# Two chunks of 256 tokens beside the first MLP become one of 512 with its output in two passes

## The chip, the cores and the metric

The kernel runs on one core of a Trainium2 chip. The metric is the device time of one execution in microseconds; each version is run several times and the median is given.

## The reference, cut to what matters

```python
def _attn_ref(q, k, v, omega):             # q, k, v: (4, 8, 576, 64), omega: (128, 64)
    ...
    q_p, k_p = (phi(q_s), phi(k_s))        # random features with exp
    kv = np.einsum('bhsm,bhsd->bhmd', k_p, v)
    z = np.sum(k_p, axis=2)
    num = np.einsum('bhsm,bhmd->bhsd', q_p, kv)
    den = np.einsum('bhsm,bhm->bhs', q_p, z)[..., None] + 1e-06
    return (num / den).astype(np.float32)

def _moe_ref(x, w_in, w_out, alpha):       # x: (2304, 512), d_ff 2048
    h = x @ w_in
    g = np.maximum(h, 0.0) + alpha * np.minimum(h, 0.0)
    return (g @ w_out).astype(np.float32)

def _moe2_ref(x, w_a, w_b, w_out):         # d_ff 1536
    ...
    return (a * b @ w_out).astype(np.float32)
```

The result is attention, then the first MLP, then the second, for 2304 tokens of 512 features, all in float32. The change lies in the first MLP alone.

## The kernel before, in words

Every float32 matrix product is made of three products of high and low halves: a value's high half is its float32r rounding, made on ScalarE (`xh`, `gh`, the high half of a weight), its low half is the value less that, made on VectorE or POOL (`xl`, `gl`). TensorE sums high x high, high x low and low x high.

The first MLP has 16 tiles of 128 hidden features, numbered f, in two phases of 8. Phase 0 takes f 0 to 7 for all tokens and writes partial sums to the memory tile `ypart`; phase 1 takes f 8 to 15, reads `ypart` (`load_y`, line 652), adds and writes it back. For one chunk of tokens and one f, `h` is 12 matmuls (4 tiles of input features, 3 products each); ScalarE takes `u` from it, VectorE multiplies and adds (`u<-u,bend,h`), ScalarE makes `gh`, VectorE `gl`; `y` is another 12 matmuls into four output tiles, which stand in PSUM until the last f.

In phase 0 the first 1280 tokens are five chunks of 256 (`CI`, `NCI`), worked on while attention still runs; `work0` (lines 1107 and 1108) lists them. Chunks 0 and 1 are done by `A.run`. From there `group` (line 1048) sets the order of work, written out by hand: a group is two steps of attention (projections `pp`, `kv`, `nd` for numerator and denominator, transposes `tp` and `xp`, with their copies) and up to two items of the list `line`: the `y` of the pair before, put between the transposes, then two `h` (`Mlp.whole`, line 576). `whole` leaves the making of `gh` and `gl` to a list `after` that the next group flushes in its middle. When attention has no steps left, `h` and `y` alternate without it. The last y of a chunk leaves PSUM through a tile `yo` of the pool `io`, which has one buffer (line 499), and a store on SP's queue (lines 638 to 644).

After the last chunk `over()` (line 1100) closes attention's pools, opens the pools of the 512-token stage and issues its first two splits, `xh_1280_0`, `xl_1280_0`, `xh_1280_1`, `xl_1280_1`; only then is the last `y` of the chunk at token 1024 popped from the queue (lines 1171 and 1172). The stage for tokens 1280 to 2303 and phase 1 follow, then the second MLP.

The weights come as float32 bits in DRAM and are decoded into halves by `Decoder`. During the chunks of 256 there are 17 free slots for decoded weights (`NS1`); further ones open with the 512-token stage.

Of the kernel before, what the change touches and what calls it, by code (L numbers as in the profile page):

```python
# [9 lines left out]
F32 = mybir.dt.float32  # L10
F32R = mybir.dt.float32r
# [7 lines left out]
P = 128  # L19
# [39 lines left out]
PACE3 = 1  # L59
FIRST = 32  # L60
ALONE = 4
LAND = 5.0
SIDE = 0

# [2 lines left out]
def tile_kernel(ctx: ExitStack, tc: tile.TileContext, qT, kT, v1, omT, wbits, alpha, out):  # L67
# [145 lines left out]
    class Decoder:  # L213
# [255 lines left out]
    def hilo(q):  # L469
        D_.upto(q)  # L470
        return slots[place(q)][:2]
# [5 lines left out]
    class Mlp:  # L477
# [98 lines left out]
        def whole(self, ph, o, n, f, last):  # L576
# [18 lines left out]
            self.after.append(rest)  # L595
            self.q.append((self.a_back, ph, o, n, f, last))

        def a_back(self, ph, o, n, f, last_chunk):
# [12 lines left out]
            gh, gl = self.gs.pop((ph, o, f))  # L611
            for e in range(KT):
                es = slice(e * P, (e + 1) * P)
                head = not self.pair or e % 2 == 0
                tail = not self.pair or e % 2 == 1
                for i, (w_, r_) in enumerate(((wh, gh), (wh, gl), (wl, gh))):
                    tensor.matmul(ys[e], lhsT=w_[:, es], rhs=r_,
                                     start=(first and i == 0 and head), stop=(last and i == 2 and tail))
                if not self.pair and e < 3 and not last:
                    D_.fill()  # L620
            D_.free[2 * f + 1] = last_chunk
            if last:
# [386 lines left out]
    with st_m:  # L1009
# [35 lines left out]

        wait = {}

        def group(fronts, at):

            s = nxt_s[0]  # L1050
            nxt_s[0] += 2
            D_.step(2 * DEC1)
# [12 lines left out]
            if kv:  # L1065
                a_kv(*kv.pop(0))
            spread(fronts, KT)
# [10 lines left out]
            spread(line[at:at + 5], 2)  # L1078
            D_.go(5)
            for i in range(2):  # L1080
                if i < len(t):
                    a_t(*t[i])
                    wait["num"].append(t[i])
                if full:
                    A.back_one(fronts, 2 - i)
            for w in fronts:
                A.whole(*w)
                if not full:
                    A.back_one(fronts)
            D_.go(3)  # L1090

        def more():
            return nxt_s[0] < last_q or any(wait.values())
# [11 lines left out]


        work0 = [(0, CI * i, CI, fs, False) for fs in (range(NFH), range(NFH, NF0)) for i in range(2)]
        work0 += [(0, CI * i, CI, range(NF0), False) for i in range(2, NCI)]

        def ready(end, k):  # L1110
            b, t = divmod(end - 1, S)
# [32 lines left out]
                        most -= 1  # L1144

        i = sum(len(w[3]) for w in work0[:ALONE])
        while i < len(line):
            if not more():
                spread(line[i:i + 5], 2)
            pair = []  # L1150
            early = 1 if more() else 0
            for w in line[i:i + 2]:
                ph, o, n, f, _ = w
                if all((ph, o, k) in A.xs or x_there(o + n, k, True) for k in range(KT)) and D_.ready >= 2 * f + 2 - early:
                    pair.append(w)
            if len(pair) < 2 and more():
                pair = []
            if more():
                group(pair, i)
            else:  # L1160
                for w in pair:
                    A.flush()
                    A.whole(*w)
                    A.back_one(pair, 3)
                    D_.fill()
# [345 lines left out]
```

## Time and profile before

| | |
|---|---|
| median of 3 runs | 946.66 us (946.53 to 946.99) |
| the profiled execution | 947.25 us, span 945.5 us |
| mean granted clock of TensorE | 0.998 of full speed |
| busy share of the span | TensorE 98%, VectorE 65%, ScalarE 54%, POOL 13% |
| the chain that ended last | TensorE 93%, ScalarE 3%, VectorE 2% |

The span goes from the first to the last instruction of the profiled execution; its own time is 1.75 us longer. Busy shares are means over stages with different limits, so what a change in one stage is worth is read from that stage's waits. In the rows, PE is TensorE, DVE VectorE, ACT ScalarE, SPq the queue of SyncE; `L189` is a helper that records every matmul and most VectorE instructions, so groups are told apart by tile names.

### The profile page before, as it was taken

Reading aid. Unit: us, or ns where it says so; the run is one execution under the profiler, and the core shown is the slowest. Engines: PE = TensorE matmul, PEld = TensorE weight load, DVE = VectorE, ACT = ScalarE, POOL = GpSimd, SP = SyncE. Lnnn points to the kernel's source line nnn. Section 1 sums busy time; section 2 is a strip of 40 time slices with the busy share of each in tenths; the row PEclk is TensorE's granted clock in tenths of the full one; section 3 lists DMA queues with packets and bytes.
Section 4 is the critical chain, followed back from the end, with each engine's and each line's share of the span. In section 5 each row is a group of like instructions: output and inputs, shape, how many; then the busy total and the mean of one; then the engine's idle time right before and its main releaser. Section 6 shows DMA issues by size and latency. Waiting matters only on the chain.

```text
span 945.5 us, 16672 instructions
## 1 busy us (share of the span) xinstructions
PE 930.3 (98%) x6483; PEld 842.1 (89%) x6483; DVE 610.0 (65%) x1248; ACT 508.5 (54%) x1195; POOL 125.5 (13%) x107
## 2 busy tenths in 40 slices
PE   7989999999999999999999999999999999999998
PEld 6779999989888888889888999999999998989896
DVE  4987875653567677678776786866486833373633
ACT  5977766543455555445444556555465542444541
POOL 2786700000001202000000000000011111110201
PEclk9999999999999999999999999999999999999999
DMA  8444322000233352356546856159828368323323
GB/s 304 173 165 169 148 81 70 3 24 24 68 99 124 89 179 67 123 189 222 189 167 257 281 220 241 59 214 386 310 49 255 52 191 273 109 36 98 54 48 68
DMA packets 49566, 138.92 MB, mean 147 GB/s; under 512 B 4560, under 2 KB 11088, under 8 KB 49488
## 3 DMA queue, kind: packets, MB, share of 16 engines
q1 hardware_dynamic: 44592, 129.08, 38.4%
q0 software_dynamic: 4752, 8.65, 6.3%
q8 instruction: 51, 0.84, 0.4%
q14 instruction: 27, 0.22, 0.1%
q10 hardware_dynamic: 144, 0.13, 0.0%
HBM read 90.66 MB, written 47.19 MB: 146 GB/s over the span
## 4 chain that ended last, share of the span: by engine, by line
PE 93%; ACT 3%; DVE 2%; issue 1%; DMA 1%; ACTq 0%
PE y L189 21%; PE h L189 20%; PE W L189 16%; PE o L189 16%; PE E L189 8%; PE B L189 4%; ACT ph L811 2%; PE tp L189 2%; PE kv L189 2%; PE nd L189 1%; DMA raw<-in_w 1%; PE xp L189 1%; ACT r L257 0%; DVE xl L518 0%; PE warm L189 0%
## 5 line engine op out<-in xcount | busy, mean ns | idle before, releaser
L189 PE MATMUL y<-gh,w 128*128 128x256 f32 (+1 forms) x768 | 203.4, 339 | 0.0
L189 PE MATMUL h<-xh,w 128*128 128x256 f32 (+1 forms) x768 | 189.1, 338 | 2.0 <-DVE gl L189 0.8
L189 PEld LDWEIGHTS y<-gh,w 128*128 128x128 f32 x768 | 134.8, 189 | 14.9
L189 PEld LDWEIGHTS h<-xh,w 128*128 128x128 f32 x768 | 125.7, 189 | 18.1 <-DVE gl L189 1.0
L189 PE MATMUL o<-w,gh 128*128 128x512 f32 x432 | 133.1, 389 | 0.0
L189 PE MATMUL y<-gl,w 128*128 128x512 f32 (+1 forms) x384 | 129.0, 336 | 0.6 <-DVE gl L189 0.6
L189 PE MATMUL h<-xl,w 128*128 128x512 f32 (+1 forms) x384 | 109.7, 336 | 0.2 <-DVE xl L518 0.2
L189 PEld LDWEIGHTS o<-w,gh 128*128 128x128 f32 x432 | 81.0, 188 | 16.5
L189 DVE SCALAR_TENSOR_TENSOR h<-u,bend,h 128x512 f32<-128x512 f32 (+1 forms) x72 | 47.8, 664 | 56.6 <-ACT u L552 56.5
L189 PE MATMUL o<-w,gl 128*128 128x512 f32 x216 | 84.2, 390 | 0.0
L1410 POOL DMA_DIRECT2D out<-op x30 | 26.3, 875 | 421.6 <-ACT op L164 340.8
L189 PEld LDWEIGHTS y<-gl,w 128*128 128x128 f32 x384 | 72.7, 189 | 8.4 <-DVE gl L189 0.8
L564 ACT ACTIVATE gh<-h 128x512 fp32r<-128x512 f32 (+1 forms) x72 | 38.0, 527 | 63.8 <-DVE h L189 63.8
L189 PEld LDWEIGHTS h<-xl,w 128*128 128x128 f32 x384 | 64.3, 189 | 7.9 <-DVE xl L518 0.4
L552 ACT ACTIVATE u<-h 128x512 f32<-128x512 f32 (+1 forms) x72 | 37.9, 526 | 56.2 <-PE h L189 52.5
L518 POOL TENSOR_TENSOR xl<-xT,xh 128x512 fp32r<-128x512 f32 (+1 forms) x16 | 20.2, 1272 | 341.8 <-ACT xh L514 341.8
L164 ACT ACTIVATE u<-W 128x384 f32<-128x384 f32 x72 | 35.3, 493 | 50.2 <-PE W L189 47.1
L164 ACT ACTIVATE op<-o 128x512 f32<-128x512 f32 x51 | 30.5, 597 | 58.1 <-PE o L189 45.1
L189 DVE TENSOR_TENSOR u<-E,u 128x384 f32<-128x384 f32 x36 | 19.6, 554 | 52.3 <-PE E L189 49.2
L189 DVE TENSOR_TENSOR gl<-h,gh 128x512 fp32r<-128x512 f32 (+1 forms) x72 | 43.1, 598 | 15.9 <-ACT gh L564 15.1
L189 DVE CUSTOM_DVE_ANT_0 a<-a,r 128x1024 uint16<-128x1024 uint16 x68 | 49.5, 727 | 4.2
L189 PEld LDWEIGHTS o<-w,gl 128*128 128x128 f32 x216 | 40.5, 188 | 8.5
(497 smaller groups left out, 1967.1 us busy)
## 6 DMA issues: line engine op xcount, KB each, us to landing
raw<-in_w SPq DMA_DIRECT2D x68, 512.0 KB, 4.6
w<-store SPq DMA_DIRECT2D x45, 512.0 KB, 6.8
store<-t_None SPq DMA_DIRECT2D x40, 512.0 KB, 3.8
st<-ypart SPq DMA_DIRECT2D x14, 768.0 KB, 8.0
out<-op POOLq DMA_DIRECT2D x30, 256.0 KB, 5.1
q<-in_qT SPq DMA_DIRECT2D x8, 576.0 KB, 3.8
v<-in_v SPq DMA_DIRECT2D x7, 650.0 KB, 5.9
yp<-ypart SPq DMA_DIRECT2D x4, 1024.0 KB, 6.1
```

The source lines that it names most:

```text
L164: nc.scalar.activation(out, in_, AF.Copy)
L189: return call(*a, **k)
L518: (nc.vector, nc.gpsimd)[way].tensor_tensor(out=lo, in0=src, in1=hi.bitcast(F32), op=ALU.subtract)
L552: nc.scalar.activation(u_, hp, AF.Relu, scale=-1.0)
L564: nc.scalar.activation(gh, hp, AF.Copy)
L811: nc.scalar.activation(ph[:, 2 * pr + j], pair[j][:, o + pr], AF.Exp, bias=nm[:, j, o + pr:o + pr + 1])
L1410: nc.gpsimd.dma_start(out=dst, in_=op, accum_op=ALU.add)
```

## The change

The chunks at tokens 768 and 1024 leave the list, and one chunk of 512 tokens (`WIDE` = 768) takes their place, written out after the loop. Its halves of x (`wide_split`) stand in tiles of the weight decoder's pool, its `gh` and `gl` in attention's buffers for k, v and one of the features (`hold`). PSUM has room for two of its four output tiles at a time, so `y` is made for output tiles 0 and 1 over f 0 to 3, then 2 and 3 over f 0 to 3, and both pairs again over f 4 to 7. Each pair leaves through the pool `io` (`wide_leave`): over f 0 to 3 with a store on SP's queue, over f 4 to 7 with an accumulating DMA on POOL's queue, which adds to `ypart` in memory. A group takes one `h` of 512 columns in place of two of 256. `over()` comes after the whole chunk has left.

```diff
+WIDE = 768
...
+        def wide_front(self, o, f, hold):
+            hilo(2 * f + 1)
+            wh, wl = hilo(2 * f)
+            hp = self.psh.tile([P, 512], F32, tag=self.htag, name=f"hw{o}_{f}")
...
+                    tensor.matmul(hp, lhsT=w_[:, k * P:(k + 1) * P], rhs=self.xs[0, o, k][low],
+                                  start=(i == 0), stop=(i == 3 * KT - 1))
...
+            for c in range(2):
+                cs = slice(c * CI, (c + 1) * CI)
+                u_ = self.pu.tile([P, CI], F32, tag="u", name=f"uw{o}_{f}{c}")
+                nc.scalar.activation(u_, hp[:, cs], AF.Relu, scale=-1.0)
+                vector.scalar_tensor_tensor(out=u_, in0=u_, scalar=bend[:, f:f + 1], in1=hp[:, cs],
+                                            op0=ALU.mult, op1=ALU.add)
+                us.append((cs, u_))
...
+        def wide_leave(self, o, es, outs, add):
+            yo = self.io.tile([P, KT, CI], F32, tag="io", name=f"yw{o}_{es[0]}{add}").rearrange("p (e c) n -> p e (c n)", c=2)
+            nc.scalar.activation(yo[:, 0], outs[0], AF.Copy)
+            vector.tensor_copy(yo[:, 1], outs[1])
+            dst = ypart[:, es[0]:es[0] + 2, o:o + 2 * CI]
+            if add:
+                nc.gpsimd.dma_start(out=dst, in_=yo, accum_op=ALU.add)
+            else:
+                nc.sync.dma_start(out=dst, in_=yo)
...
-        work0 += [(0, CI * i, CI, range(NF0), False) for i in range(2, NCI)]
+        work0 += [(0, CI * i, CI, range(NF0), False) for i in range(2, NCI - 2)]
...
+        lo_e, hi_e = (0, 1), (2, 3)
+        plan = [[A.pop, A.pop], [y_of([0], lo_e, True, False)], [y_of([1], lo_e, False, False)],
+                [y_of([2], lo_e, False, False)], [y_of([3], lo_e, False, True)],
+                [y_of([0, 1, 2, 3], hi_e, True, True)], [y_of([4, 5], lo_e, True, False)]]
+        for f, ys in enumerate(plan):
+            group(ys, [lambda f=f: A.wide_front(WIDE, f, hold)])
         A.flush()
         while more():
-            group([], i)
+            group([], [])
+        A.wide_front(WIDE, 7, hold)
+        y_of([4, 5, 6], hi_e, True, False, pool=True)()
+        A.flush()
+        y_of([6, 7], lo_e, False, True, True)()
+        y_of([7], hi_e, False, True, True)()
+        assert not A.q
         over()
         while A.q:
             A.pop()
```

How the order moves, first on ScalarE at the handover from the last narrow or wide chunk to the 512-token stage. Names in brackets are the semaphores that an instruction waits for (DMAHW: a transfer of SP's queue, DMASW: one of POOL's). Before:

```order
L591 ACTIVATE gh_1024_6_4008<-u_1024_6_3993 128x256 [waits DVE_49]
L584 ACTIVATE u_1024_7_4025<-h_1024_7_4012 128x256 [waits PE_49,Activation_49]
L591 ACTIVATE gh_1024_7_4040<-u_1024_7_4025 128x256 [waits DVE_49]
L514 ACTIVATE xh_1280_0_4052<-xT 128x512 [waits DMAHW6_49,DMAHW4_49,DMAHW2_49]
L514 ACTIVATE xh_1280_1_4056<-xT 128x512 [waits DMAHW6_49,DMAHW5_49]
L643 ACTIVATE yo_4084<-y_1024_0_3863 128x256 [waits DMAHW2_49,PE_49]
L643 ACTIVATE yo_4084<-y_1024_1_3864 128x256 [waits PE_49]
L514 ACTIVATE xh_1280_2_4123<-xT 128x512
L514 ACTIVATE xh_1280_3_4127<-xT 128x512
```

The same place on ScalarE after the change:

```order
L634 ACTIVATE gw_7_3809<-uw_70_3783 128x256
L634 ACTIVATE gw_7_3809<-uw_71_3786 128x256 [waits DVE_49]
L649 ACTIVATE yw_0True<-yw_6_3751 128x512 [waits DMAHW3_49,PE_49]
L649 ACTIVATE yw_2True<-yw_3789 128x512 [waits DVE_49,DMASW0_49,PE_49,Activation_49]
L515 ACTIVATE xh_1280_0_3848<-xT 128x512 [waits PE_49]
L515 ACTIVATE xh_1280_1_3852<-xT 128x512 [waits DMAHW6_49]
L515 ACTIVATE xh_1280_2_3889<-xT 128x512
L515 ACTIVATE xh_1280_3_3893<-xT 128x512
L553 ACTIVATE u_1280_0_3913<-h_1280_0_3897 128x512 [waits DVE_49,DMASW1_49,PE_49,Activation_49]
```

The first two `xh` of the next stage stood ahead of the copies of the last output; now they stand behind both copies of the accumulated output, of which the second waits for a transfer of POOL's queue, and the stage's first `u` waits for the other one.

Second, TensorE in the group in which the last steps of queries are projected (`pp(7, 4)`). Before:

```order
L189 MATMUL h_768_5_3567<-xh_768_1_2864,w_88 128x256
L189 MATMUL h_768_5_3567<-xh_768_2_3044,w_88 128x256
L189 MATMUL h_768_5_3567<-xh_768_3_3048,w_88 128x256
L189 MATMUL xp_1_3583<-ident,xn_1_3455 128x128 x2
L189 MATMUL xp_2_3587<-ident,xn_2_3469 128x128 x2
L189 MATMUL nd_3_3591<-kvp_168,phT_3_3520 64x65 x8
L189 MATMUL nd_4_3605<-kvp_168,phT_4_3537 64x65 x4
L189 MATMUL pp(7, 4)_True_3623<-xT,q_2824 128x128
L189 MATMUL pp(7, 4)_True_3624<-xT,q_2824 128x128
L189 MATMUL tp_2_3641<-ident,ph_2_3488 128x128 x4
L189 MATMUL y_768_0_3370<-gh_768_4_3615,w_87 128x256
L189 MATMUL y_768_0_3370<-gl_768_4_3616,w_87 128x256
```

The same group on TensorE after the change:

```order
L190 MATMUL hw_2_3472<-xw_2_3042,w_82 128x512
L190 MATMUL hw_2_3472<-xwh_3_3045,w_82 128x512
L190 MATMUL xp_1_3491<-ident,xn_1_3405 128x128 x2
L190 MATMUL xp_2_3495<-ident,xn_2_3419 128x128 x2
L190 MATMUL nd_3_3499<-kvp_168,phT_3_3459 64x65 x8
L190 MATMUL nd_4_3513<-kvp_168,phT_4_3470 64x65 x4
L190 MATMUL pp(7, 4)_True_3528<-xT,q_2824 128x128
L190 MATMUL pp(7, 4)_True_3529<-xT,q_2824 128x128
L190 MATMUL tp_2_3538<-ident,ph_2_3435 128x128 x4
L190 MATMUL yw_1_3351<-gw_2_3523,w_83 128x512 x3
L190 MATMUL yw_1_3355<-gw_2_3523,w_83 128x512 x3
L190 MATMUL tp_3_3551<-ident,ph_3_3449 128x128 x4
```

The attention between `h` and `y` is the same; 24 narrow matmuls of `y` per group (12 of each f, with a transpose between) have become 6 wide ones, and the `y` reads the halves of the one `h` just ahead.

## Rows read from the trace of the kernel before

**Rows 1.** The page, part 1: busy time, share of the span, instructions
```profile
PE 930.3 (98%) x6483; PEld 842.1 (89%) x6483; DVE 610.0 (65%) x1248; ACT 508.5 (54%) x1195; POOL 125.5 (13%) x107
```

**Rows 2.** Stretches: length, busy time (instructions) by engine, PEclk, DMA share, GB/s
```profile
200.00:250.00 50.00, 49.09 (x466) 47.17 (x462) 24.50 (x69) 20.80 (x60) 0.00 (x0) 1.00 0.05 18
...
262.00:531.00 269.00, 269.00 (x1279) 226.63 (x1278) 193.58 (x329) 138.37 (x259) 20.19 (x16) 1.00 0.47 160
531.00:940.00 409.00, 409.00 (x2159) 383.48 (x2158) 244.58 (x486) 204.02 (x429) 28.93 (x33) 1.00 0.52 161
```

**Rows 3.** TensorE's waits in 100 to 262 us: total, times, longest
```profile
PE y L189 <- DVE gl L189: 0.6, 1, 0.6
PE h L189 <- DVE yo L189: 0.2, 1, 0.2
```

**Rows 4.** The chain that ended last, in order of time: start, us, what
```profile
215.35 2.88 PE h L189 x24
...
255.72 2.72 PE y L189 x12
```

**Rows 5.** Timeline of TensorE, attention groups: start, us, what, idle before
```profile
202.86 0.28 PE L189 MATMUL y<-gl,w 128*128 128x256 f32 x1
...
210.91 0.36 PE L189 MATMUL y<-gh,w 128*128 128x256 f32 x1
...
211.91 0.39 PE L189 MATMUL y<-gl,w 128*128 128x256 f32 x1 [0.63 <-DVE gl L189]
```

**Rows 6.** Timeline of VectorE in the same groups
```profile
202.05 0.75 DVE L189 TENSOR_TENSOR gl<-u,gh 128x256 fp32r<-128x256 f32 x2
...
209.38 0.48 DVE L189 SCALAR_TENSOR_TENSOR u<-u,bend,h 128x256 f32<-128x256 f32 x1 [0.96 <-ACT u L584]
...
211.44 0.75 DVE L189 TENSOR_TENSOR gl<-u,gh 128x256 fp32r<-128x256 f32 x2
```

**Rows 7.** Timeline of TensorE at the start of the 512-token stage
```profile
247.25 0.50 PE L189 MATMUL h<-xh,w 128*128 128x512 f32 x1 [0.22 <-DVE yo L189]
```

**Rows 8.** Timeline of ScalarE at the start of the 512-token stage
```profile
244.07 1.14 ACT L514 ACTIVATE xh<-xT 128x512 fp32r<-128x512 f32 x2
...
252.06 0.60 ACT L552 ACTIVATE u<-h 128x512 f32<-128x512 f32 x1 [3.57 <-DMA ypart<-yo]
```

**Rows 9.** Timeline of VectorE: a copy and a split of 512 columns
```profile
166.41 0.68 DVE L189 COPY phT<-tp 128x512 f32<-128x512 f32 x1
...
244.72 1.29 DVE L518 TENSOR_TENSOR xl<-xT,xh 128x512 fp32r<-128x512 f32 x2
```

**Rows 10.** Timeline of ScalarE near the end, about 794 to 803 us
```profile
793.97 0.60 ACT L164 ACTIVATE op<-o 128x512 f32<-128x512 f32 x1 [3.10 <-PE o L189]
...
802.73 0.60 ACT L164 ACTIVATE op<-o 128x512 f32<-128x512 f32 x1 [5.44 <-DMA out<-op]
```

**Rows 11.** Timeline of POOL at the same place
```profile
794.98 0.87 POOL L1410 DMA_DIRECT2D out<-op  x1 [33.70 <-ACT op L164]
```

**Rows 12.** DMA issues, us to landing: whole span; then at 749, 795, 798 us
```profile
ypart<-yo SPq DMA_DIRECT2D x2, 1024.0 KB, 5.3
...
ypart<-yo SPq DMA_DIRECT2D x3, 512.0 KB, 3.2
...
out<-op POOLq DMA_DIRECT2D x1, 256.0 KB, 3.9
...
out<-op POOLq DMA_DIRECT2D x1, 256.0 KB, 7.7
...
out<-op POOLq DMA_DIRECT2D x1, 256.0 KB, 8.9
```

**Rows 13.** Timeline of TensorE near the beginning
```profile
14.56 1.18 PE L189 MATMUL kv<-v,ph 128*64 128x65 f32 x16 [2.47 <-ACT ph L811]
```

**Rows 14.** Stretches near the beginning, columns as in rows 2
```profile
15.00:15.50 0.50, 0.50 (x12) 0.50 (x12) 0.00 (x0) 0.50 (x4) 0.18 (x1) 0.50 1.01 318
...
18.00:18.50 0.50, 0.50 (x16) 0.44 (x12) 0.50 (x2) 0.00 (x0) 0.50 (x1) 0.83 0.97 398
```

More of the change, by code (lines that the diff above doesn't have):

```diff
@@ L596, in whole, with wide_split @@
             self.q.append((self.a_back, ph, o, n, f, last))
+        def wide_split(self, o, k):
+            src = xT[:, k, o:o + 2 * CI]
+            if k < KT - 1:
+                t = dec.tile([P, 2, 512], F32R, tag="t", name=f"xw{o}_{k}", bufs=3)
+                hi, lo = t[:, 0], t[:, 1]
+            else:
+                hi, lo = [dec.tile([P, 512], F32R, tag="a", name=f"xw{c}{o}_{k}", bufs=3) for c in "hl"]
+            nc.scalar.activation(hi, src, AF.Copy)
+            vector.tensor_tensor(out=lo, in0=src, in1=hi.bitcast(F32), op=ALU.subtract)
+            self.xs[0, o, k] = (hi, lo)
@@ new lines, in wide_front, with rest @@
+        def wide_front(self, o, f, hold):
+            hilo(2 * f + 1)
+            wh, wl = hilo(2 * f)
+            hp = self.psh.tile([P, 512], F32, tag=self.htag, name=f"hw{o}_{f}")
+            i = 0
+            for w_, low in ((wh, 0), (wh, 1), (wl, 0)):
+                for k in range(KT):
+                    tensor.matmul(hp, lhsT=w_[:, k * P:(k + 1) * P], rhs=self.xs[0, o, k][low],
+                                  start=(i == 0), stop=(i == 3 * KT - 1))
+                    i += 1
+            load["act"] += 1.6
+            load["dve"] += 2.0
+            us = []
+            for c in range(2):
[5 more added lines that the diff above has]
+                us.append((cs, u_))
+            def rest():
+                gh, gl = hold(f"{o}_{f}")
+                for cs, u_ in us:
+                    nc.scalar.activation(gh[:, cs], u_, AF.Copy)
+                for cs, u_ in us:
+                    vector.tensor_tensor(out=gl[:, cs], in0=u_, in1=gh[:, cs].bitcast(F32), op=ALU.subtract)
+                self.gs[0, o, f] = (gh, gl)
+            self.after.append(rest)
@@ new lines, in wide_y @@
+        def wide_y(self, o, f, e, out, first, last):
+            wh, wl = hilo(2 * f + 1)
+            gh, gl = self.gs[0, o, f]
+            for i, (w_, r_) in enumerate(((wh, gh), (wh, gl), (wl, gh))):
+                tensor.matmul(out, lhsT=w_[:, e * P:(e + 1) * P], rhs=r_, start=(first and i == 0), stop=(last and i == 2))
+        def wide_leave(self, o, es, outs, add):
[5 more added lines that the diff above has]
+                nc.gpsimd.dma_start(out=dst, in_=yo, accum_op=ALU.add)
+            else:
+                nc.sync.dma_start(out=dst, in_=yo)
@@ L1046, in tile_kernel, with group @@
         wait = {}
-        def group(fronts, at):
+        def group(ys, hs, first=lambda: None, mid=lambda: None):
             s = nxt_s[0]
             nxt_s[0] += 2
-            D_.step(2 * DEC1)
             full = s < last_q
@@ L1066, in group @@
                 a_kv(*kv.pop(0))
-            spread(fronts, KT)
+            first()
             A.flush()
@@ L1077, in group @@
                     wait["t"].append(ev["q"][x])
[L1078 to L1083, printed above, removed]
-                if full:
[L1085 to L1090, printed above, removed]
+            mid()
+            D_.go(8)
+            ys, hs = list(ys), list(hs)
+            for ut in t:
+                a_t(*ut)
+                wait["num"].append(ut)
+                if full and ys:
+                    ys.pop(0)()
+            for h in hs:
+                if full:
+                    while ys:
+                        ys.pop(0)()
+                h()
+                if not full and ys:
+                    ys.pop(0)()
+            for y in ys:
+                y()
         def more():
@@ L1146, in tile_kernel, with mid @@
         i = sum(len(w[3]) for w in work0[:ALONE])
+        wide_k = list(range(KT))
         while i < len(line):
-            if not more():
+            pair = line[i:i + 2]
+            for ph, o, n, f, _ in pair:
+                assert all((ph, o, k) in A.xs or x_there(o + n, k, True) for k in range(KT)) and D_.ready >= 2 * f + 2
+            def mid():
                 spread(line[i:i + 5], 2)
[L1150 to L1165, printed above, removed]
-            i += len(pair)
+                if i + 4 >= len(line):
+                    for k in wide_k[:2]:
+                        assert x_there(WIDE + 2 * CI, k)
+                        A.wide_split(WIDE, k)
+                    del wide_k[:2]
@@ new lines, in tile_kernel, with hold @@
+            group([A.pop] * 2, [lambda w=w: A.whole(*w) for w in pair], lambda: spread(pair, KT), mid)
+            i += len(pair)
+        kv_bufs = [("k", 2 * S), ("v", TT * VC)]
+        def hold(nm):
+            n = n_hold[0]
+            n_hold[0] += 1
+            if n == 4:
+                return [pk.tile([P, 4, M], F32R, tag="k", name=f"gw{c}{nm}").rearrange("p a m -> p (a m)") for c in "hl"]
+            tag, size = kv_bufs[(n - (n > 4)) % 2]
+            t = ld.tile([P, size], F32R, tag=tag, name=f"gw{nm}")
+            return t[:, :512], t[:, 512:1024]
@@ new lines, in tile_kernel, with y_bank, y_of, go @@
+        n_hold = [0]
+        outs = {}
+        def y_bank(e, pool=None):
+            if pool:
+                return bank(f"yw{e}")
+            return A.psy.tile([P, 2, 256], F32, tag="y", name=f"yw{e}_{n_hold[0]}").rearrange("p c n -> p (c n)")
+        def y_of(fs, es, first, last, add=False, pool=None):
+            def go():
+                for e in es:
+                    if first:
+                        outs[e] = y_bank(e, pool)
+                    for f in fs:
+                        A.wide_y(WIDE, f, e, outs[e], first and f == fs[0], last and f == fs[-1])
+                if last:
+                    A.wide_leave(WIDE, es, [outs.pop(e) for e in es], add)
+            return go
```

## The prediction

> **What bounds the kernel now.** I read the page first: TensorE is busy 98% of the span [rows 1]. Then the stretches: it is busy 49.09 of 50 us around the change, and in 262 to 940 us it is busy for the whole time [rows 2], so no idle time exists later that could swallow a delay or give room to a gain: what this stage gains or loses reaches the end. Then the waits of TensorE in 100 to 262 us: 0.6 us on a low half `gl` and 0.2 us at the start of the 512-token stage [rows 3]. So the change can win only matmul time, and any wait that it adds is lost in full. The sum is made against the profiled execution of 947.25 us; that lies 0.59 us above the median of 946.66, and I add the difference to the median.
>
> **What it saves.** Two chunks of 256 tokens need 2 x 8 x 24 = 384 matmuls of 256 columns. The chain shows 24 of them in 2.88 us, 120 ns each [rows 4]: 46.08 us. The chunk of 512 needs 192 of 512 columns; twelve take 2.72 us, 226.7 ns each [rows 4]: 43.52 us. **Saved: 2.56 us.** The Trainium skill ("TensorE: Matmul & The Clock Gate", Back-to-back issue gap) gives a matmul N / 2.4 ns plus 2.5, an estimate of 109 and 216 ns and so a gain of 0.5 us only, which would make the sum 2.1 us worse; the rows are 11 ns above it at both widths, and I go by them.
>
> **What it adds inside the attention groups.** A group now runs one wide `h` instead of two narrow ones, and `y` needs both halves of its low part. The last narrow pair let ScalarE begin on the first `h` while TensorE made the second; now both halves begin after the whole `h`. VectorE's two steps on `u`, of which the later stands at 209.38 with 0.48 us [rows 6], then follow directly on each other behind the whole `h`, and the later one ends some 0.4 us after its present time. In the group at 202 us VectorE runs without a break to the two `gl` (202.05, 0.75 for both [rows 6]), so they end at 203.2 in place of 202.8, and the `y` that reads them could start at 202.97 (0.107 us later than the 202.86 of the row [rows 5], its predecessor being wider): a wait of 0.25 us. In the group at 211 us TensorE already waits 0.63 us [rows 5]: the two `gl` began at 211.44 [rows 6], both are needed, so the matmul of 211.91 moves by 0.4 for the step and 0.35 for the second half: 0.75 us more. The group before these gets relief, since two copies of `xT` leave VectorE for ScalarE, and in the later ones `y` stands behind another 2.72 us of `h`. **Added: 1.0 us**, between 0 (the wider `h` ends 0.16 us sooner and the covers hold) and 2 (each of four groups as bad as half of these).
>
> **What it adds at the handover to the 512-token stage.** This decides. The four results of the wide chunk leave through one tile: the pool `io` has one buffer, and each `yw` takes all of it. The last two leave directly behind each other, 6 matmuls apart (1.36 us). The order shows the second copy on ScalarE waiting for DMASW0, the software queue's transfer of the first, and `xh_1280_0`, which the next stage's first matmul needs, stands behind that copy. Before, the first two `xh` stood ahead of the output's copies.
>
> The same wait stands in the trace elsewhere: ScalarE's copy at 802.73 sat 5.44 us idle for an accumulating transfer [rows 10] issued by POOL at 794.98 [rows 11], which landed after 7.7 us [rows 12], at 802.68. From the end of the first pair's matmuls (call it 0):
> - VectorE's copy of 512 columns takes 0.68 us [rows 9]; POOL's issue starts 0.41 us after a copy's end (793.97 + 0.60 against 794.98 [rows 10, 11]): issue at 1.15 with 0.05 us to start.
> - Landing of 512 KB with an add is not in the trace. 256 KB of that kind took 3.9 us where nothing else ran and 8.9 in the busiest place [rows 12]. Plain stores of 512 and 1024 KB took 3.2 and 5.3 us [rows 12], 1.05 per 256 KB more. From 3.9 that gives 5.0; twice 3.9 gives 7.8, if nothing in it is fixed. I take 6.0, nearer to the lower because part is fixed, and keep 3.9 and 8.9 for the range. Landed at 7.15. (The skill, "DMA: Bandwidth & Descriptors", Anatomy of one DMA, fits 2.0 us plus bytes over 436e3: an estimate of 3.2 us, and a sum 2.8 us lower. The same fit gives 2.6 us for 256 KB, where the rows show 3.9 to 8.9.)
> - ScalarE's copy from 7.2; `xh` follows after 0.55 and takes 0.57 us (two in 1.14 [rows 8]); TensorE can start at 8.4. Its own work ended at 1.36, so it idles 7.0 us, where it idled 0.22 [rows 7]: **6.8 us added**. The second matmul waits for the first `xl`, 0.65 us [rows 9] behind `xh`: another 0.25 us.
> - The clock: at 14.56 TensorE returned from 2.47 us idle [rows 13], and the granted clock was 0.50 (1.2 of 2.4 GHz) then and until about 18.2 [rows 14], so 3.6 us of work went at half rate. A longer idle time will do the same: **1.8 us added**, between 0 and 2.5.
>
> ScalarE's first `u` of the next stage waits for the second accumulating transfer, as it waited 3.57 us for the store before [rows 8]. That transfer is issued at 8.3 (7.2 + 0.68 + 0.41) and lands near 14.3. `y` of this stage is first due at about 18.6 (three `h` of 2.72 us from 8.4, plus 0.25 and the clock's 1.8), and `gl` is ready some 2.8 us behind `u` (a copy, a step, a copy and a subtraction of about 0.7), at 17.1: covered by 1.5 us; what a landing takes over 7.5 us is lost.
>
> **What costs nothing.** The splits of `x` have as many columns as before and lie beside the matmuls of the same groups; they use the weight decoder's tiles, and the decoder stands still there, having no free slot until the next stage. Its loads on SP, queued behind the last store before, now start sooner, but no wait on them is among TensorE's. POOL gets two issues, one `xl` of chunk 512 and nothing that anyone waits for except the above. The accumulated columns are read again only some 100 us later.
>
> **Sum.** -2.56 + 1.0 + 6.8 + 0.25 + 1.8 = +7.3 us: 954.0 us on the median, 954.5 for an execution like the profiled one. About 0.2% (1.9 us) is what a measurement can tell from no change, so this is slower.
>
> **Rivals.**
> - *A short handover.* The transfer lands as the quiet 256 KB did (3.9) and the clock stays up: -2.1 - 1.8 + 0.2 (the wait for `xl` is no longer shared with slow matmuls) makes +3.6, 950.3 us. For it: the DMA queues are nearly idle here. Against: twice the bytes, and a shorter idle time already cost the clock [rows 13, 14].
> - *A long handover.* 8.9 us to land, and the second one exposes `u` by 1.4: +7.3 + 2.9 + 1.4 = +11.6, 958.3 us. For it: the rows of 7.7 and 8.9 [rows 12]. Against: those ran beside loads.
> - *No wait on the transfer (not slower).* If the second copy is free to start when its matmuls end, the handover costs only copy to `xh` to matmul: 0.1 + 0.55 + 0.57 + 0.1 - 0.22 = 1.1, plus 0.4 for `xl`, and no idle time long enough for the clock: -2.56 + 1.0 + 1.5 = -0.1, 946.6 us; without the waits in the groups -1.1. It decides where the tile isn't shared, or from a landing of 2.2 us down with the clock up (-2.56 + 1.0 + 0.8 + 2.2 + 0.4 = 1.9). Against: the order names the wait, [rows 10, 11] show it holding, and no such transfer in [rows 12] landed in under 3.9 us.
> - *The matmuls save more, or nothing.* That the change does what it says, the order settles (192 matmuls of 512 columns for 384). Faster by over 1.9 us needs a free handover and free groups at once.
>
> **How the numbers follow.** Forecast 0.72, short handover 0.13, long 0.10, no wait 0.05. Slower by over 0.2% holds in the first three: 0.95. The no-wait case gives 0.04 to no change and 0.01 to faster. The range runs from 949.8 (short handover with the groups at 0.5) to 958.6 (long one, clock at its upper end) and leaves out some 0.1 to 0.15.
>
> **What would show it.** In the changed profile: 24 wide `y` or `h` matmuls in 5.44 us; a TensorE idle time of about 7 us before the first `h` of chunk 1280, in which ScalarE's second `yw` copy is put down to the DMA `ypart<-yw`; a granted clock of 0.50 for 3 to 4 us behind it; waits of some 0.3 and 1.4 us on `gl` in two groups. Wrong would be: that idle time under 3 us, or TensorE idle time appearing elsewhere, after 262 us above all.

## Result, and the profile after

The changed kernel takes **959.82 us** (median; 959.15 to 960.84), the kernel before 946.83 us on the same chip: ratio **1.0138 [1.0120, 1.0156]**, 13.0 us slower. The forecast was 7.3 us slower, and the result lies 1.2 us above the end of its range. The profiled execution took 959.15 us, with a span of 957.2 us.

The page of the changed kernel, part 1, answers to [rows 1]:

```profile
PE 932.9 (97%) x6291; PEld 834.5 (87%) x6291; DVE 610.1 (64%) x1241; ACT 507.8 (53%) x1193; POOL 128.5 (13%) x110
```

192 matmuls fewer are in the trace (6291 for 6483), yet TensorE is busy 2.6 us longer, and the span is 11.7 us longer. The matmuls that a slower clock stretched are in the first number; the rest is idle time. Where it lies, the stretches tell (length, busy time by engine with instructions, granted clock, DMA share, GB/s), against [rows 2]:

```profile
240.00:250.00 10.00, 9.22 (x40) 7.12 (x38) 2.42 (x5) 2.09 (x5) 0.84 (x1) 1.00 0.00 1
250.00:272.00 22.00, 15.63 (x56) 12.44 (x57) 10.89 (x17) 7.78 (x14) 1.77 (x2) 0.77 0.33 48
...
272.00:540.00 268.00, 268.00 (x1275) 225.80 (x1274) 191.58 (x327) 139.05 (x259) 20.98 (x17) 1.00 0.46 157
550.00:951.00 401.00, 401.00 (x2116) 375.76 (x2115) 237.35 (x472) 199.97 (x420) 28.59 (x33) 1.00 0.52 158
```

As before, nothing after the stage's start has room: TensorE is busy without a gap, so what is lost before 272 us reaches the end. TensorE's waits in 100 to 262 us (total, times, longest), against [rows 3]:

```profile
PE h L190 <- ACT xh L515: 7.2, 1, 7.2
PE yw L190 <- DVE gw L190: 1.0, 1, 1.0
PE nd L190 <- ACT kvp L890: 0.8, 1, 0.8
PE pp(7, 4)_True L190 <- ACT xT L946: 0.5, 1, 0.5
PE pp(7, 3)_True L190 <- DVE rc L190: 0.3, 1, 0.3
PE tp L190 <- ACT xT L946: 0.3, 1, 0.3
PE pp(7, 2)_True L190 <- ACT xT L946: 0.2, 1, 0.2
PE tp L190 <- PE pp(6, 4)_True L190: 0.2, 1, 0.2
```

Two things are to be seen: one wait of 7.2 us where 0.2 us stood, and seven short ones, 3.3 us together, where there were two, 0.8 together: the 0.6 of [rows 3] and, in the kernel before, this one:

```profile
PE tp L189 <- DVE xn L189: 0.2, 1, 0.2
```

**The handover.** TensorE, ScalarE and POOL around it, by their timelines (start, us, what, idle before and what ended it), against [rows 7, 8]:

```profile
256.37 0.79 PE L190 MATMUL h<-xh,w 128*128 128x512 f32 x1 [7.15 <-ACT xh L515]
```

```profile
246.46 0.60 ACT L649 ACTIVATE yw_0True<-yw 128x512 f32<-128x512 f32 x1 [3.32 <-PE yw L190]
255.21 0.60 ACT L649 ACTIVATE yw_2True<-yw 128x512 f32<-128x512 f32 x1 [8.15 <-DMA ypart<-yw_0True]
255.70 2.18 ACT L515 ACTIVATE xh<-xT 128x512 fp32r<-128x512 f32 x4
262.54 0.60 ACT L553 ACTIVATE u<-h 128x512 f32<-128x512 f32 x1 [4.66 <-DMA ypart<-yw_2True]
```

```profile
249.16 1.39 POOL L653 DMA_DIRECT2D ypart<-yw_0True  x1 [132.18 <-DVE yw_0True L190]
```

and the DMA issues there (us from issue to landing):

```profile
ypart<-yw_0True POOLq DMA_DIRECT2D x1, 512.0 KB, 5.9
```

POOL issues the first pair's transfer at 249.16; it lands 5.9 us later; only then may ScalarE's second copy take the one `io` buffer; the four `xh` follow it, and TensorE's first `h` the first of these. The first `u` waits 4.66 us for the second transfer, but no wait of TensorE comes from that. Behind the idle time the clock is at half (columns as above):

```profile
252.00:256.00 4.00, 0.00 (x0) 0.00 (x0) 0.69 (x1) 0.80 (x2) 0.00 (x0) 0.50 0.65 111
256.00:260.00 4.00, 3.63 (x8) 2.61 (x9) 3.10 (x5) 1.88 (x4) 1.23 (x1) 0.50 0.46 50
260.00:264.00 4.00, 4.00 (x15) 3.19 (x14) 0.83 (x2) 0.64 (x2) 0.00 (x0) 0.72 0.46 83
264.00:268.00 4.00, 4.00 (x19) 3.31 (x18) 2.82 (x5) 2.46 (x5) 0.00 (x0) 1.00 0.00 0
```

0.50 is 1.2 of 2.4 GHz. In 260 to 264 us a mean of 0.72 is half for 2.2 us and full for the rest: the clock was back at about 262.2, 5.8 us after TensorE's return.

**The groups.** ScalarE and VectorE behind a wide `h` that ended at about 198.7 us:

```profile
198.78 0.38 ACT L626 ACTIVATE uw<-hw 128x256 f32<-128x256 f32 x1 [1.82 <-PE hw L190]
199.72 0.38 ACT L626 ACTIVATE uw<-hw 128x256 f32<-128x256 f32 x1 [0.55 <-DVE uw L190]
200.00 0.38 ACT L946 ACTIVATE xT<-xp 128x256 f32<-128x256 f32 x1
```

```profile
199.20 0.48 DVE L190 SCALAR_TENSOR_TENSOR uw<-uw,bend,hw 128x256 f32<-128x256 f32 x1 [4.17 <-ACT uw L626]
200.13 0.48 DVE L190 SCALAR_TENSOR_TENSOR uw<-uw,bend,hw 128x256 f32<-128x256 f32 x1 [0.45 <-ACT uw L626]
```

ScalarE in the same group of the kernel before:

```profile
197.98 0.38 ACT L584 ACTIVATE u<-h 128x256 f32<-128x256 f32 x1 [1.94 <-PE h L189]
199.42 0.38 ACT L584 ACTIVATE u<-h 128x256 f32<-128x256 f32 x1 [1.06 <-PE h L189]
199.80 0.38 ACT L887 ACTIVATE xT<-xp 128x256 f32<-128x256 f32 x1
```

Before, each Relu copy waited for its own `h`, and `xT` came 0.38 us after the second. Now the second copy waits 0.55 us for VectorE's step on the *first* half: copy, step, copy, step run one after another, 1.83 us (198.78 to 200.61), and the attention's `xT` stands behind them.

**Ledger**, from the starts of TensorE's rows (after against before):

| where | us |
|---|---|
| all `h` and `y` matmuls of the last 512 narrow tokens, idle time taken out: 47.21 to 45.69 | -1.5 |
| `nd` and `pp` of four groups 2.41, 2.59, 1.27, 1.08 to 3.13, 3.52, 2.03, 1.48, and `gl`/`gw` 0.63 to 1.03 | +3.2 |
| idle time at the handover, 0.22 to 7.15 | +6.9 |
| first `h` of chunk 1280 to its first `y`, 8.31 to 11.18 (clock, and waits for `xl`) | +2.9 |
| the program's start (a wait at 14 us, 2.47 to 3.27 us, not touched by the change) | +0.3 |

That is 11.8 for 11.7 us. The wait at the start differs from execution to execution of any kernel: over the 14 kernels profiled here TensorE's first `pp(4, 0)` matmul begins between 74.97 and 77.68 us, and from there the steps up to the first wide group come alike within 0.02 us. It blurs medians by a microsecond or so. So the experiments are read twice: by the ratio, and by the **rest**, the span less that start (one profiled execution each), which is 869.3 us before and 880.7 after: **+11.4 us**.

### The profile page after: what moved, and what is told of

It is laid out like the page before. It is cut to its first block, busy times and chain, and to the rows that moved or that the text cites. A ratio compares the mean times of both kernels' runs of the same rounds, so it can differ in the third digit from the quotient of the medians.

```text
span 957.2 us, 16284 instructions
## 1 busy us (share of the span) xinstructions
PE 932.9 (97%) x6291; PEld 834.5 (87%) x6291; DVE 610.1 (64%) x1241; ACT 507.8 (53%) x1193; POOL 128.5 (13%) x110
## 4 chain that ended last, share of the span: by engine, by line
PE 73%; DMA 1%; ACT 0%; DVE 0%; issue 0%; ACTq 0%
PE W L190 16%; PE o L190 15%; PE h L190 15%; PE y L190 15%; PE E L190 8%; PE B L190 4%; DMA ypart<-yw_0True 1%; DVE held L190 0%; ACT yw_2True L649 0%; ACT xh L515 0%; ACTq L649 0%
## 5 line engine op out<-in xcount | busy, mean ns | idle before, releaser
L190 PE MATMUL h<-xh,w 128*128 128x512 f32 (+1 forms) x640 | 171.1, 352 | 8.9 <-ACT xh L515 7.9
L190 PE MATMUL y<-gh,w 128*128 128x512 f32 (+1 forms) x640 | 177.7, 349 | 0.0
L190 PEld LDWEIGHTS h<-xh,w 128*128 128x128 f32 x640 | 109.7, 191 | 25.5 <-ACT xh L515 8.5
L190 PEld LDWEIGHTS y<-gh,w 128*128 128x128 f32 x640 | 113.9, 189 | 15.0
L190 PE MATMUL y<-gl,w 128*128 128x512 f32 (+1 forms) x320 | 110.8, 346 | 0.0
L190 PE MATMUL h<-xl,w 128*128 128x512 f32 (+1 forms) x320 | 100.5, 350 | 0.2 <-DVE xl L519 0.2
L190 PEld LDWEIGHTS y<-gl,w 128*128 128x128 f32 x320 | 60.4, 189 | 7.5
L190 PEld LDWEIGHTS h<-xl,w 128*128 128x128 f32 x320 | 56.1, 191 | 8.5 <-DVE xl L519 0.8
```

The source lines that it names most:

```text
L190: return call(*a, **k)
```

## The experiments

Two questions: is the handover the one buffer's doing, at the price named; and what makes the groups three times as dear as forecast? Ratios are to the kernel before on the same chip.

| kernel | ratio [interval] | rest, us |
|---|---|---|
| before | | 869.3 |
| the change | 1.0138 [1.0120, 1.0156] | 880.7 |
| two tiles | 1.0026 [1.0014, 1.0038] | 873.4 |
| two tiles, splits first | 1.0030 [1.0019, 1.0041] | 872.3 |
| plain store | 1.0086 [1.0062, 1.0110] | 878.4 |
| dummy matmuls | 1.0101 [1.0073, 1.0128] | 878.7 |
| copies back | 1.0136 [1.0120, 1.0152] | 882.4 |
| before, copies moved | 0.9995 [0.9986, 1.0004] | 869.1 |
| narrow h | 1.0086 [1.0070, 1.0102] | 877.7 |
| relus first | 1.0101 [1.0086, 1.0116] | 879.2 |
| before, splits last | 1.0015 [1.0006, 1.0024] | 870.6 |
| two tiles, narrow h | 1.0007 [0.9998, 1.0017] | 869.8 |
| two tiles, relus first | 1.0022 [1.0013, 1.0032] | 870.5 |
| all four repairs | 1.0003 [0.9993, 1.0014] | 869.3 |

### The handover

**Two tiles.** The second pair of outputs gets a tile of the idle weight decoder.

```diff
-            yo = self.io.tile([P, KT, CI], F32, tag="io", ...)
+            if add and es[0]:
+                yo = dec.tile([P, 2, 512], F32R, tag="t", ..., bufs=3).bitcast(F32)
+            else:
+                yo = self.io.tile([P, KT, CI], F32, tag="io", ...)
```

> The second accumulated pair leaves through another tile, so its copy no longer waits for the first pair's transfer; all else is as in the change. Theory (one shared tile): TensorE's idle time before the first h of chunk 1280 falls from 7.15 us to about 1.3 (a copy of 0.6 and a split of 0.57), the granted clock stays at 1.00 behind it, and the time falls by some 8 us, from 959.8 to about 952. Rival (the transfer itself, or the splits standing behind the copies, costs the time): the idle time stays over 5 us and the time over 957.

Measured: 950.54 us. The idle time of 7.15 us is gone; the two transfers still take 6.2 and 6.1 us, and nothing waits for them that counts. TensorE and ScalarE in its trace:

```profile
250.14 0.50 PE L190 MATMUL h<-xh,w 128*128 128x512 f32 x1 [0.72 <-ACT xh L515]
```

```profile
248.76 0.60 ACT L652 ACTIVATE yw_2True<-yw 128x512 f32<-128x512 f32 x1 [1.50 <-PE yw L190]
```

The rest falls by 7.3: 6.4 of idle time and 2.4 of the slow clock (first `h` to first `y` takes 8.78 instead of 11.18), while 1.6 is lost at another place, where the clock fell behind the 1.03 us wait for `gw`:

```profile
210.00:214.00 4.00, 3.38 (x11) 2.80 (x12) 0.96 (x4) 1.53 (x4) 0.00 (x0) 0.65 0.02 4
214.00:218.00 4.00, 4.00 (x44) 3.19 (x45) 0.48 (x1) 0.68 (x3) 0.00 (x0) 0.92 0.00 0
```

(`y`, a transpose and the next `h` took 3.32, 0.71 and 3.56 us there, against 2.78, 0.36 and 2.82 in the change's own trace, where the same wait left the clock at 1.00.) The buffer and its transfer are the handover's cause.

**Two tiles, splits first.** The same, with the next stage's splits ahead of the last copies.

```diff
+                if last == "over":
+                    over()
                 if last:
                     A.wide_leave(WIDE, es, [outs.pop(e) for e in es], add)
...
-        y_of([7], hi_e, False, True, True)()
-        assert not A.q
-        over()
+        y_of([7], hi_e, False, "over", True)()
+        assert not A.q
```

> As the two tiles, and the first two splits of the next stage stand ahead of the last pair's copies. Theory: another 0.5 us, about 951.5, idle time before h under 1 us. Rival (the order of splits and copies is what costs): most of the 8 us comes only here, the run with two tiles alone showing little.

Measured: 950.74 us, no gain; a miss. The first `h` waits 0.72 us as before. The rest is 1.1 us lower only because here the clock stayed up behind the wait for `gw` (1.6), while first `h` to first `y` took 0.5 longer. In the changed kernel, with the tile free, the order of splits and copies is worth nothing that can be measured (in the kernel before, see below, it is worth 1.3 us).

**Plain store.** The second half goes out by SP without an add; so the first four feature tiles' share of the last 512 narrow tokens is left out of the result.

```diff
-            if add:
+            if False:
                 nc.gpsimd.dma_start(out=dst, in_=yo, accum_op=ALU.add)
```

> The second passes are stored over the first ones on SP's queue in place of being added to them by POOL's queue, so the chunk's output lacks the first four features' sum; one tile as in the change. Theory (the landing of the transfer sets the idle time): a store of 512 KB lands in 3.2 to 4.0 us where the add took 5.9, so the idle time falls by 2 to 3 us to 4 to 5 us; the clock still falls; 956 to 957.5. Rival (software queue as such is what costs): idle time near 1.3 us, about 952.

Measured: 955.95 us. The transfer landed after 2.7 us, not 5.9, and the idle time fell with it by 3.75 us, to less than the 4 to 5 us expected:

```profile
254.91 0.80 PE L190 MATMUL h<-xh,w 128*128 128x512 f32 x1 [3.40 <-ACT xh L515]
```

```profile
ypart<-yw_0True SPq DMA_DIRECT2D x1, 512.0 KB, 2.7
```

The landing sets the idle time. The clock was at half behind 3.40 us just as behind 7.15 (first `h` to first `y` 11.24 us), and once more in the group (0.89 and 0.69 in 210 to 218 us), which makes up the difference between 3.75 and the 2.3 by which the rest fell.

**Dummy matmuls.** 26 matmuls of 512 columns that nobody reads fill most of the idle time.

```diff
         assert not A.q
+        w_ = bank("dummy")
+        gh, gl = A.gs[0, WIDE, 7]
+        for i in range(26):
+            tensor.matmul(w_, lhsT=hilo(15)[0][:, :P], rhs=gh, start=True, stop=True)
         over()
```

> 26 matmuls of 512 columns that nobody reads, about 5.9 us, stand behind the chunk's last matmul, where TensorE idles; else as the change. Theory (the idle time lets the clock fall, which costs 2.2 to 2.6 us behind it): the first h of chunk 1280 starts at the same time, the clock stays at 1.00, and the time falls by about 2.3 us to 957.5. Rival (the slow start of the stage comes from the supply of splits): the time stays at 959.8.

Measured: 957.37 us; the first `h` starts as late as in the change, but at full clock:

```profile
257.53 0.50 PE L190 MATMUL h<-xh,w 128*128 128x512 f32 x1 [1.16 <-ACT xh L515]
```

```profile
258.00:264.00 6.00, 5.78 (x26) 4.75 (x26) 2.61 (x5) 1.08 (x3) 0.89 (x1) 1.00 0.61 87
```

First `h` to first `y` is 8.82 us, 2.36 less than in the change: that is the clock's price by itself. The rest falls by 2.0 only, since 0.4 us is lost behind it: with the clock up the first `gl` of the stage, whose `u` still waits for the second transfer, comes too late for the second `y` matmul (0.41 us behind the first, not 0.23).

### The attention groups

After the first trace I had a theory that the forecast's words on copies of `xT` leaving VectorE seemed to ask for: the kernel's `pick`, which gives each copy to the engine with less work by its own estimate, had moved ten copies between ScalarE and VectorE (four of `phT` and `xT` to VectorE, six of `xT` to ScalarE), and these stood ahead of `kvp`.

**Copies back**, and **before, copies moved.** A table puts each of the ten on the engine it had before; in the other kernel the same table, with the engines exchanged, is all that is done to the kernel before.

```diff
+MOVED = {("t", 5, 3): 0, ("t", 6, 0): 0, ("t", 7, 0): 0, ("x", 6, 4): 0, ("x", 4, 3): 1, ("x", 4, 4): 1, ...}
...
-        if pick({"act": 0.2 + n / 600}, {"dve": 0.1 + n / 480}):
+        way = pick({"act": 0.2 + n / 600}, {"dve": 0.1 + n / 480})
+        if MOVED.get(("x", u, t), way):
```

> The change, with the ten copies of attention results that changed between ScalarE and VectorE put back on the engine they had before; all else as in the change. Theory (moved copies hold up kvp and with it nd): TensorE's wait of 0.8 us on kvp goes, and about half of the four short waits on xT and rc (1.3 us together) with it; the time comes 1.0 to 1.5 us below the change, ratio to the kernel before 1.0120 to 1.0125. Rival (the wide h itself, with all its u work following at once, crowds ScalarE and VectorE, whichever engine copies): the waits stay at 2.5 to 3.3 us in sum and the time within 0.4 us of the change. The wait on gw (1.0 us) and the handover (7.1 us) stay in both.

> The kernel before, with the ten copies moved between ScalarE and VectorE as the change moves them, and nothing else. Theory (the moved copies are what holds up kvp): waits of nd on kvp of 0.4 to 0.8 us appear, and the time rises by 0.5 to 1.2 us, ratio 1.0005 to 1.0013. Rival (they do harm only beside the wide h): no wait over 0.3 us appears, and the time stays within 0.3 us of the kernel before.

Measured: 960.81 us and 947.37 us; the theory fell twice. With the copies back the wait on `kvp` shrank (0.3 for 0.8), those on `xT` and `rc` stayed, and one on `xn` came:

```profile
PE pp(7, 4)_True L191 <- ACT xT L949: 0.5, 1, 0.5
...
PE nd L191 <- ACT kvp L891: 0.3, 1, 0.3
...
PE tp L191 <- DVE xn L191: 0.3, 1, 0.3
```

`nd` and `pp` of the four groups took 10.34 us, in the change 10.16. And the moved copies in the kernel before made no wait at all. (The rest of 882.4 holds a fall of the clock behind `gw`, as in the two-tile run.)

**Narrow h.** Each wide `h` is made in two halves of 256 columns, each in its own PSUM bank; `y` stays wide.

```diff
-            hp = self.psh.tile([P, 512], F32, tag=self.htag, name=f"hw{o}_{f}")
...
+            for c in range(2):
+                cs = slice(c * CI, (c + 1) * CI)
+                hp = self.psh.tile([P, 512], F32, tag=self.htag, name=f"hw{o}_{f}{c}")[:, :CI]
...
+                        tensor.matmul(hp, lhsT=w_[:, k * P:(k + 1) * P], rhs=self.xs[0, o, k][low][:, cs], ...)
```

> The change, with each h of the wide chunk made in two halves of 256 columns, each in a bank of its own, so that u's steps on the first half run beside the second; y stays wide. Theory (late u after the whole wide h causes the waits on gw): the wait on gw falls from 1.0 to under 0.3 us; the narrow h costs 8 x (2.88 - 2.72) = 1.3 us of matmul time, so that the time stays within 0.7 us of the change, a little above it if the other waits stay as they are. Rival (gw is late because VectorE is behind with other work): the wait stays above 0.7 us and the time rises by 1.0 to 1.5 us. The handover stays at 7.1 us in both.

Measured: 955.44 us, where no gain was expected; the size of it was the surprise that settled the matter. Its waits in 100 to 262 us, all of them:

```profile
PE h L190 <- ACT xh L515: 7.2, 1, 7.2
PE yw L190 <- DVE gw L190: 0.9, 1, 0.9
PE tp L190 <- DVE xn L190: 0.2, 1, 0.2
```

`nd` and `pp` take 2.40, 2.59, 1.28 and 1.08 us, the values of the kernel before to 0.01. The wait on `gw`, at which the edit was aimed, stayed (0.85 for 1.03). The narrow `h` cost 0.11 us each (2.97 for 2.86), under 1 us in all. So the price of the groups was the wide `h` in one bank: the `u` work on it, not the copies, made `xT`, `kvp` and `rc` late. The edit changes two things at once, a bank for each half and an earlier start of the first half; the next run takes away only the second copy's wait for VectorE.

**Relus first.** `h` stays wide, but both Relu copies of `u` are issued ahead of VectorE's two steps, so that the second no longer waits for the first step.

```diff
                 nc.scalar.activation(u_, hp[:, cs], AF.Relu, scale=-1.0)
+                us.append((cs, u_))
+            for cs, u_ in us:
                 vector.scalar_tensor_tensor(out=u_, in0=u_, scalar=bend[:, f:f + 1], in1=hp[:, cs],
                                             op0=ALU.mult, op1=ALU.add)
-                us.append((cs, u_))
```

> The change, with the two Relu copies of u issued ahead of the two steps of VectorE, so that the second copy no longer waits for the first step; the wide h stays. Theory (the chain copy, step, copy, step on one bank, 1.83 us behind each wide h, holds up xT and kvp on ScalarE and rc on VectorE): the second copy starts 0.3 us behind the first instead of 0.94, the waits of pp on xT and rc and of nd on kvp fall from 2.3 us together to under 1.0, and the time comes 1.5 to 3 us below the change, ratio to the kernel before 1.0105 to 1.012. Rival (with narrow h it was the 1.44 us head start of the first half that helped): the waits stay over 1.8 us and the time is within 0.7 us of the change. The handover stays at 7.1 us in both.

Measured: 956.39 us. ScalarE and TensorE's waits:

```profile
205.78 0.66 ACT L626 ACTIVATE uw<-hw 128x256 f32<-128x256 f32 x2 [1.39 <-PE hw L190]
206.33 0.39 ACT L947 ACTIVATE xT<-xp 128x256 f32<-128x256 f32 x1
```

```profile
PE yw L190 <- DVE gw L190: 1.0, 1, 1.0
PE pp(7, 3)_True L190 <- DVE rc L190: 0.3, 1, 0.3
PE tp L190 <- DVE xn L190: 0.2, 1, 0.2
```

The two copies now follow each other at once, `xT` starts 0.55 us behind the first (1.22 in the change), and the waits on `xT` and `kvp` are gone. `nd` and `pp` take 8.60 us, against 10.16 and 7.35 before: the order of four instructions was half of the loss. What the narrow `h` gains beyond that can be the earlier start of the first half or VectorE's freedom from the bank that ScalarE reads (here its first step still starts behind the second copy); no run parts the two.

### Order alone, and what the repairs are worth together

**Before, splits last.** The kernel before, with `over()` behind the last output copies.

```diff
-        over()
         while A.q:
             A.pop()
+        over()
```

> The kernel before, with the splits of the next stage's first chunk placed behind the copies of the last narrow outputs, as the change places them. Theory (order counts only where a copy waits for a transfer): the first h of chunk 1280 waits 0.7 to 1.5 us in place of 0.22, no transfer is named, the clock stays at 1.00, and the time is 0.5 to 1.3 us above the kernel before. Rival (the order alone makes the handover expensive): an idle time of over 3 us and the clock at half behind it, 5 us or more.

Measured: 949.39 us; the first `h` waits 0.99 us for `xh` and the second matmul 0.23 for `xl`, with the clock at 1.00. The order alone costs 1.3 us by the rest; it is the transfer that makes it 7.

**Two tiles with narrow h**, and **two tiles with relus first**: the edits above, put together.

> The change with both repairs: the second pair of outputs in a tile of its own, and each h of the wide chunk in two halves of 256 columns; y stays wide. Theory (the handover and the late halves of u are separate costs and add): second tile about -10.5 us, narrow h about -4.7 us against the change, ratio to the kernel before 0.997 to 0.9995, 0.5 to 3 us under it. Rival (the narrow h gained through the state of the clock at the handover, not in the groups): ratio 1.0015 to 1.003, no better than the second tile alone.

> The change with the second pair of outputs in a tile of its own and the two Relu copies of u ahead of VectorE's steps; h and y both wide. Theory: waits in the groups of 1.0 to 1.8 us in place of 3.3, and the matmul time of the wide h kept (some 1 us less than with narrow h): ratio to the kernel before 0.998 to 1.001. Rival (relus first does nothing): ratio 1.0025, that of the second tile alone.

Measured: 948.66 and 949.46 us. The first lands above its expectation: it ties with the kernel before instead of beating it. By the rest, 880.7 falls by 10.9 to 869.8. The narrow `h` alone gave 3.0 and the second tile 8.9 (7.3, and 1.6 that the clock took back in a group), together 11.9; 1.0 of it counts twice, since behind the handover the narrow `h`'s trace lost only 1.4 us to the clock (10.22 less 8.82). So the two costs are separate and add, to within 0.1 us; the expectation's 10.5 us for the second tile came from the medians of two separate comparisons. The second misses too: 1.0022 lies above its 0.998 to 1.001 and at its rival's 1.0025, and by the ratio it can't be told from the second tile alone (1.0026). Its trace does show the gain, `nd` and `pp` at 8.6 us for 10.16, and a rest 2.9 us lower, of which 1.6 is the clock's fall in the other run. The narrow `h` beats relus first by 0.7 us in the rest.

**All four repairs**: two tiles, narrow `h`, the splits ahead of the last copies, and in the fourth wide group `y` behind `h`.

```diff
-            group(ys, [lambda f=f: A.wide_front(WIDE, f, hold)])
+            if f == 3:
+                group([], [lambda f=f: A.wide_front(WIDE, f, hold)] + ys)
+            else:
+                group(ys, [lambda f=f: A.wide_front(WIDE, f, hold)])
```

> The change with the second pair of outputs in a tile of its own, each h of the wide chunk in two halves, the splits of the next stage's first chunk ahead of the last outputs' copies, and in the fourth wide group y behind h instead of ahead of it. Theory (the four costs add): from 0.5 us above the kernel before (two tiles and narrow h, the start of the program taken out), 0.85 us less for the wait on gw and about 1.1 us less for the splits: 1 to 2 us under the kernel before by the trace, ratio 0.9978 to 0.9995. Rival (the wait on gw only moves to the next reader, and the first y of the next stage waits for what its gl stands behind): ratio 1.000 to 1.001.

Measured: 948.11 us beside 947.92: a tie, where 1 to 2 us under the kernel before were expected. The wait on `gw` is gone and nothing took its place: TensorE's waits in 100 to 262 us are 0.7 on `xh`, 0.2 on `xl` and 0.2 on `xn`.

Where the saving goes, the starts of TensorE's rows tell. From the first wide `h` to the first `h` of chunk 1280 this kernel takes 60.31 us and the kernel before 60.96 for the same work, the longer wait at `xh` included; from there to the first `y` it takes 9.23 us, the kernel before 8.31, and what was won is gone. The other run with the splits first shows 9.26 there, also with the clock up; why it is longer was not tried apart. No version beat the kernel before.

## Why the prediction was right, and where wrong

**Right: direction, mechanism, place.** Full busyness later, the single buffer, ScalarE's second copy held by the first transfer, `xh` behind it: all stand in the trace. The handover was put at 6.8 us from a landing of 6.0; it is 6.93 with a landing of 5.9. The 6.0 was picked between two extrapolations, 5.0 and 7.8, so that it came within 0.1 us is in part luck; the wait for the landing is not. The Trainium skill's fit ("DMA: Bandwidth & Descriptors", Anatomy of one DMA), cited in the prediction for an estimate of 3.2 us, is made for transfers from GpSimd's queue, POOL's in the rows; the accumulating transfers on that queue took 5.8 to 6.3 us here. Covered as foretold: the late `u` of the next stage, the splits in the decoder's tiles, the decoder's loads.

**Wrong: the groups, +1.0 forecast, +3.2 measured, the largest miss.** The failed step is "VectorE's two steps on `u` ... then follow directly on each other behind the whole `h`, and the later one ends some 0.4 us after its present time". In truth the second Relu copy waited for the first step: the chain ended 1.83 us behind the start of the first copy, not 1.34 (0.38 + 2 x 0.48). And I followed only `gl`, while ScalarE's next work, `xT` and `kvp`, stood behind the chain too. Of the 1.0 us forecast on `gl`, 0.4 came: in the group at 211 us the wait grew from 0.63 to 1.03, not to 1.38, and that of 0.25 at 202 us did not come. The other 2.8 us lie in `nd` and `pp`, which the forecast put at nothing. The prediction's "relief" in one group is not in the trace; the runs with the copies put back or moved show that those copies mattered little either way. The trace puts the second copy's wait of 0.55 us down to VectorE's step; the prediction has no such wait. The Trainium skill ("PSUM — Partial Sum Buffer", PSUM bank collisions raise a hardware error) says that the compiler's scheduler adds a dependency between any two instructions on different engines that touch the same bank and the same 32 partitions, reads and writes alike; the trace agrees, with 0.94 us from the start of one copy to the start of the next in one bank, where two that follow directly take 0.66 together. What put the wait into this program no run shows.

**Wrong: the saving, 2.56 forecast, 1.5 measured.** The failed step is "twelve take 2.72 us, 226.7 ns each" for matmuls of another stage: the wide `y` goes at 0.2333 us (24 in 5.60), as here, where starts 0.23 us apart and the next `h` 2.80 us behind are to be seen:

```profile
235.11 0.40 PE L190 MATMUL yw<-gwh,w 128*128 128x512 f32 x1
235.34 0.40 PE L190 MATMUL yw<-gwl,w 128*128 128x512 f32 x1
...
237.91 0.85 PE L190 MATMUL hw<-xw,w 128*128 128x512 f32 x3
```

and a wide `h` takes 2.75 to 2.89 for twelve. The narrow matmuls were dearer than their row too, 47.21 us for 46.08, but the wide ones by more, 45.69 for 43.52. Why `y` is slower was not tried apart. The Trainium skill's 109 and 216 ns ("TensorE: Matmul & The Clock Gate", Back-to-back issue gap), which gave 0.5, were too low for both widths; the truth lay between it and my rows.

**Under-sized: the clock, 1.8 forecast, 2.4 measured** (11.18 less 8.78 with the clock up). The step "3.6 us of work went at half rate" took its size from another place; here the clock was at half for 5.8 us behind TensorE's return. (At that place too the row was read a little long: the mean of 0.76 in 14.50 to 15.00 us leaves the clock up until about 14.76, so 3.4 us.) The wait for `xl` and what goes with it made 0.47 for 0.25.

Together: 2.2 + 1.06 + 0.6 + 0.2 + 0.1 (the handover) makes 4.2 of the 5.7 us by which the difference was missed; the rest is the start (0.3 in the trace) and scatter of medians from run to run. The likeliest part of that scatter is the clock behind the wait on `gw`, seen in other kernels; only one execution of the change was profiled, so it is not shown. The upper end of the range was added up wrongly as well: the long handover's 958.3 and the clock's 0.7 (2.5 for 1.8) make 959.0, not 958.6. The result lies above that too.

## What to carry to other kernels

When two results are merged into one wider one, ask who reads the wide one: here two engines took turns on one PSUM bank and ran as a chain, and what stood behind the chain on either engine was late, not only the result itself. Where one buffer serves two results that leave directly behind each other, the price here was the landing of the first transfer plus everything queued behind the second copy, plus the clock. A saving of some 10 ns a matmul should be taken from matmuls of the same kind and place, and it is soon spent: with all four repairs, this one was worth nothing.

## What the runs showed of the hardware that was not expected

- An accumulating store of 512 KB from POOL landed after 5.8 to 6.3 us in the ten kernels that have it, the same bytes at the same place without the add from SP after 2.7 and 3.2 us; queue and add were not tried apart.
- The clock's price behind an idle time did not grow with it: first `h` to first `y` took 11.24 us behind 3.40 us of idle time, and 11.18, 10.93, 10.22 and 10.84 behind 7.15, 7.36, 7.24 and 7.36 us; with the clock up, 8.78 to 8.83 in five kernels, 9.26 and 9.23 in the two with the splits first, 8.31 in the kernel before.
- A wait of 1.03 us, the same in eight kernels, was followed by a clock at half in three of their profiles (two tiles, plain store, copies back) and not in five; it cost 1.6 us in the first of these. With the wait at 0.85 us (two kernels) or 0.63 (three, the kernel before among them) it was not seen.
